# A new opening for a fused attention and mixture-of-experts kernel: three moved steps ahead of and inside the first head

## The chip, the cores and the metric

The kernel runs on one core of a Trainium2 chip. The metric is the time of one execution on the device in microseconds (us), lower being better. TensorE (PE in the views; PEld is its weight loads) multiplies, VectorE (DVE), ScalarE (ACT) and GpSimd (POOL) do the rest, and SyncE (SP) issues the loads and stores.

## The reference

```python
# attention: 4 batches x 8 heads, 576 positions, head size 64, block-causal mask (block 64)
scores = (1 / np.sqrt(D)) * np.matmul(q, k.transpose(0, 1, 3, 2))
scores = np.where(block_i >= block_j, scores, -1000000000.0)
attn = np.exp(scores - np.max(scores, axis=-1, keepdims=True))
attn = attn / (np.sum(attn, axis=-1, keepdims=True) + 1e-09)
x = np.matmul(attn, v)                       # -> 2304 tokens of 512
# first expert layer, dense; its weights arrive as 64-bit floats' bits
x = (((x @ w1) * (x @ w2)) @ w3) @ w_out
# second layer: 8 experts of (512 x 1024, 1024 x 512), the best 2 of them per token
noisy_logits = x @ w_gate + np.log1p(np.exp(x @ w_noise)) * noise
...
out[mask] += top2_w[mask, k, None] * (np.maximum(x[mask] @ w1[e], 0.0) @ w2[e])
```

The weights of the first layer (w1, w2, w3, w_out) are stored as 64-bit numbers. The kernel turns them into 32-bit ones with three integer instructions of VectorE.

## The kernel before, in words

The program has three parts that overlap: attention, one head after the other (32 heads, numbered from 0); the first expert layer in nine chunks of 256 tokens; and the second layer by expert. Precise products are made of three fast ones: each factor is split into a high part (ScalarE, a cast) and a low part (VectorE, what the cast left out).

**A head.** `prep_h` makes Q and K ready: `hi` on ScalarE (L612 for Q, L615 for K), the low part of Q on VectorE (L614), the low part of K, `kl`, on VectorE (L617). `s_unit` multiplies them into score banks `sb` on TensorE (L644, L647 with `kl`, L646 adds the mask by a small product of `mkl` and `mkr`). `s_max` takes the negated row maxima `nm` on VectorE (L658; L661 joins the two of the last tile), and ScalarE exponentiates (L663, into `pb`). `g_unit` transposes `pb` on TensorE (L677), and copies it into `pt` on ScalarE (L681); from head 8 on VectorE makes the low part of `pt` as well (L683). `av_a` and `av_b` multiply by V (L690, L702), the result `ev` is copied (L692, L705) and stored. Score tiles 0 and 1 share a bank, tiles 2 and 3 have one each, and tile 4 has two halves of 288 columns.

**Weights of the first layer.** There are 23 pieces. Each is loaded into `stg` (two buffers), converted into `stf` by `conv64` (L548, L549, L550; one buffer), and then split into a piece `pc` (cast on ScalarE L477, low part on VectorE L481). `feed` does one step of this: it splits the piece that was converted last and converts the next.

**Filler on TensorE.** Between the steps of a head stand the products of the first layer. First w3 times w_out is made from pieces (`w_unit`, 64 units of three 128x512 matmuls, `m<-pc,pc`), then the chunks (`m<-xh,pc` with w1 and w2, later `m<-pc,gt`). All are issued by L486, L487 and L488. A unit can run only when its pieces have been split; the chunks need all the w1 and w2 pieces, which are the last to be converted.

**Order.** Head i's second half and head i+1's first half are written as a list of steps in a string, `FIRST` for i below 10 and `LATER` after it: `s0` to `s3` are scores, `c` is `feed`, `f2.9` asks for 2.9 us of filler, `g`, `a`, `b` are the second half, `h` prepares the head after next, `v` and `l` load. The loop begins with i = -1, where only the first half exists. A scheduler then lays the instructions out on each engine's queue, by priorities and by what it thinks will be ready; filler and `feed` have low priority. An engine runs its queue in order.

Of the kernel before, what the change touches and what calls it, by code (L numbers as in the profile page):

```python
# [14 lines left out]
OP = mybir.AluOpType  # L15
AX = mybir.AxisListType.X
# [46 lines left out]
ZC, NF = 3, 10  # L63
# [4 lines left out]


FIRST = "g0 g1 t f2.9 c t o g2 g3 t p s0 t t s1 s2 f2.9 c t a f2.9 t b0 t s3 h t t c b1 v l"  # L70
LATER = "g0 g1 f2.6 o g2 p t c g3 t t t s0 s1 s2 t c t a f2.6 s3 b0 t t c f2.6 c t b1 h v l"


# [4 lines left out]
def r32(ap):  # L78
    return ap.bitcast(F32)
# [385 lines left out]
class Kernel:  # L465
# [88 lines left out]
    def attention(self):  # L554
        tc, nc, a = self.tc, self.nc, self.a
        moe1 = self.moe1
        stgs = ExitStack()
        with tc.tile_pool(name="p1", bufs=1, side="right") as p1, \
# [3 lines left out]
            mk32 = p1.tile([P, 2, P], F32, name="ev")  # L562
            mkl = p1.tile([P, P], BF16, name="mkl")
            mkr = p1.tile([P, 64], BF16, name="mkr")
# [8 lines left out]
            def buf(h, shape, dt, name):  # L573

                return (px if h < H and h % 2 else p1).tile(shape, dt, name=name)
# [33 lines left out]
            def prep_h(h):  # L609
                c = hd[h]  # L610
                c.hi = buf(h, [P, 2, S], F32R, "hi")
                nc.scalar.activation(c.hi[:, 0, :], c.qk[:, 0, :], AF.Copy, scale=0.125)  # L612
                lo = c.hi[64:128, 0, :]
                nc.vector.scalar_tensor_tensor(lo, c.qk[64:128, 0, :], 0.125, r32(lo), op0=OP.mult, op1=OP.subtract)  # L614
                nc.scalar.copy(c.hi[:, 1, :], c.qk[:, 1, :])  # L615
                c.kl = buf(h, [P, S], F32R, "kl")
                (nc.vector if h < NF - 1 else nc.gpsimd).tensor_tensor(c.kl, c.qk[:, 1, :], r32(c.hi[:, 1, :]), op=OP.subtract)  # L617

            def prep_v(h):
                c = hd[h]  # L620
# [29 lines left out]
            def s_max(h):  # L650
                c = hd[h]
                pb = pbs[h < H and h % 2]
                ex = []
                for t, parts in c.tiles:
                    nm = p1.tile([P, 3], F32, name=f"nm{t}")
                    for n, (o, k0, w) in enumerate(parts):
                        w = min(w, KW[t])
                        nc.vector.tensor_reduce(nm[:, n:n + 1], o[:, 0:w], axis=AX, op=OP.max, negate=True)  # L658
                        ex.append((t, n, o[:, 0:w], k0, nm[:, 2:3] if len(parts) > 1 else nm[:, 0:1]))
                    if len(parts) > 1:  # L660
                        nc.vector.tensor_reduce(nm[:, 2:3], nm[:, 0:2], axis=AX, op=OP.min)  # L661
                for t, n, src, k0, nm in ex:
                    nc.scalar.activation(pb[t][:, k0:k0 + src.free_size()], src, AF.Exp, bias=nm, scale=1.0,  # L663
                                         accum_out=sums[:, h // H, t + n, h % H:h % H + 1])
# [55 lines left out]
            wst = {}  # L720
# [43 lines left out]
            raw = []  # L764

            conv = []

            def feed():

                with tc.high_priority(offset=PIECE_PRIO):  # L770
                    feed_half()

            def feed_half():
                if len(conv) > wst.get("split", 0):
                    _, _, i, o, _ = jobs[len(conv) - 1]
                    pc, w = self.pc[i], conv[-1].shape[-1]
                    self.split((pc[:, 0, o:o + w], pc[:, 1, o:o + w]), conv[-1], low="dve")
                    wst["split"] = len(conv)
                    moe1.conv += w // 512
                n = len(conv)  # L780
                if n < len(jobs) and wst.get("n", 0) >= jobs[n][4]:
                    conv.append(self.conv64(raw[n]))
                    if n + 2 < len(jobs):
                        raw.append(self.load64(*jobs[n + 2][:2]))

# [33 lines left out]
            tick = moe1.tick  # L819
            load(0)  # L820
            nc.sync.dma_start(mk32, a["msk"])
            nc.vector.tensor_copy(mkl, mk32[:, 0, :])
            nc.vector.tensor_copy(mkr, mk32[:, 1, 0:64])
            raw += [self.load64(*jobs[n][:2]) for n in range(2)]
            nc.sync.dma_start(self.ident, a["cst"][:, 0:128])
            feed()
            prep_h(0)
            load(1)
            load_v(0)
            feed()  # L830
            feed()

            def step(i, j, op):

# [34 lines left out]
            for i in range(-1, BH):  # L869
                if i == 2:  # L870
                    moe1.setup_load()
                elif i == 3:
                    moe1.setup()
                elif i == H:
                    pxs.close()
                    moe1.p2b = moe1.p2s.enter_context(tc.tile_pool(name="p2b", bufs=1, reuse_waits="tile"))
                if i >= H and moe1.p2c is None and moe1.conv == 40:
                    stgs.close()
                    moe1.p2c = moe1.p2s.enter_context(tc.tile_pool(name="p2c", bufs=1, reuse_waits="tile"))
                for op in (FIRST if i < NF else LATER).split():  # L880
                    step(i, i + 1, op)
            sums_out(B - 1)
            moe1.ready = B
# [243 lines left out]
```

## Time and profile before

| what | value |
|---|---|
| median of 3 runs | 1084.67 us (1081.68 to 1088.02) |
| the profiled execution's own time | 1086.31 us |
| its span, first to last instruction | 1084.5 us |
| TensorE busy | 1044.3 us, 96% |
| VectorE busy | 556.7 us, 51% |
| ScalarE busy | 495.4 us, 46% |
| GpSimd busy | 303.3 us, 28% |
| mean granted TensorE clock | 0.984 of full speed |

The engines' busy times are means over parts with different limits. The span is 1.8 us shorter than the profiled execution's time, and that execution was 1.6 us slower than the median.

### The profile page before, as it was taken

How to read it: one execution, taken by the hardware profiler on the slowest of the kernel's cores; microseconds unless marked ns; L12 is line 12 of the kernel's file. 1: busy time of each engine (PE TensorE's matmuls, PEld its weight loads, DVE VectorE, ACT ScalarE, POOL GpSimd, SP SyncE). 2: the span in 40 equal slices, each digit the busy share in tenths (PEclk: the TensorE clock that was granted, in tenths of full speed). 3: DMA queues.
4: the chain of work that ended last, by engine and by line, in shares of the span. 5: the costliest groups of instructions: out<-in, count | busy, mean ns of one | idle time of the engine just before them, and what ended most of it. 6: DMA issues, size and time to landing. Idle time of an engine off the chain costs nothing.

```text
span 1084.5 us, 17388 instructions
## 1 busy us (share of the span) xinstructions
PE 1044.3 (96%) x6588; PEld 943.4 (87%) x6588; DVE 556.7 (51%) x1211; ACT 495.4 (46%) x1163; POOL 303.3 (28%) x306
## 2 busy tenths in 40 slices
PE   6999898999999999999999999999999999999996
PEld 4787697898999989899999889889898989999885
DVE  7998899585655666443345443533333333434111
ACT  5875566665566656522224332433333333333111
POOL 1000234234342426131444234241413232120211
PEclk9999898999999999999999999999999999999998
DMA  8764877247442554322423355663535445351212
GB/s 278 245 211 164 234 215 165 71 121 160 158 111 80 155 167 92 84 80 59 79 58 113 93 133 154 185 157 98 153 100 146 108 127 127 107 117 31 39 20 33
DMA packets 79106, 136.34 MB, mean 126 GB/s; under 512 B 21181, under 2 KB 46501, under 8 KB 77861
## 3 DMA queue, kind: packets, MB, share of 16 engines
q1 hardware_dynamic: 68901, 113.98, 36.2%
q0 software_dynamic: 10112, 21.16, 10.6%
q8 instruction: 54, 0.88, 0.3%
q14 instruction: 39, 0.32, 0.1%
HBM read 103.92 MB, written 31.19 MB: 125 GB/s over the span
## 4 chain that ended last, share of the span: by engine, by line
PE 84%; DVE 5%; DMA 4%; ACT 2%; issue 2%; POOL 1%; SPq 1%; POOLq 0%; ACTq 0%; DVEq 0%
PE ph L486 13%; PE ph L487 13%; PE ph L488 13%; PE m L486 10%; PE m L488 10%; PE m L487 10%; PE av L702 4%; PE tp L677 4%; PE sb L647 2%; PE sb L644 2%; DMA v<-in_v_dram 1%; PE m L959 1%; DMA stf<-in_m_dram 1%; DVE nm L658 1%; DVE pc L481 1%
## 5 line engine op out<-in xcount | busy, mean ns | idle before, releaser
L486 PE MATMUL m<-xh,pc 128*128 128x256 f32 x576 | 165.7, 291 | 1.1 <-ACT pc L477 1.0
L487 PE MATMUL m<-xh,pc 128*128 128x256 f32 x576 | 163.9, 288 | 0.0
L488 PE MATMUL m<-xh,pc 128*128 128x256 f32 x576 | 163.0, 288 | 0.6 <-DVE pc L481 0.6
L486 PE MATMUL ph<-xt,pc 128*128 128x384 f32 (+1 forms) x512 | 156.8, 309 | 3.7 <-DVE ht L974 2.1
L487 PE MATMUL ph<-xt,pc 128*128 128x384 f32 (+1 forms) x512 | 157.8, 309 | 0.0
L488 PE MATMUL ph<-xt,pc 128*128 128x384 f32 (+1 forms) x512 | 157.6, 308 | 0.0
L974 DVE SCALAR_TENSOR_TENSOR ht<-ph,ht 128x384 fp32r<-128x384 f32 (+1 forms) x128 | 61.8, 489 | 150.5 <-ACT ht L973 147.0
L481 DVE TENSOR_TENSOR pc<-stf,pc 128x1024 fp32r<-128x1024 f32 (+1 forms) x75 | 88.2, 1191 | 93.1 <-ACT pc L477 83.6
L486 PE MATMUL ph<-pc,ht 128*128 128x512 f32 x320 | 126.0, 395 | 0.0
L488 PE MATMUL ph<-pc,ht 128*128 128x512 f32 x320 | 124.6, 390 | 0.0
L487 PE MATMUL ph<-pc,ht 128*128 128x512 f32 x320 | 124.5, 390 | 0.0
L1001 POOL DMA_INDIRECT out_dram<-yo,ids x40 | 66.5, 1661 | 207.1 <-ACT yo L997 105.8
L973 ACT ACTIVATE ht<-ph 128x384 fp32r<-128x384 f32 (+1 forms) x128 | 55.0, 438 | 136.7 <-PE ph L488 133.9
L486 PEld LDWEIGHTS m<-xh,pc 128*128 128x128 f32 x576 | 111.7, 195 | 2.4 <-ACT pc L477 1.2
L663 ACT ACTIVATE pb<-sb,nm 128x288 f32<-128x288 f32 (+3 forms) x192 | 94.1, 500 | 39.1 <-DVE nm L658 14.4
L487 PEld LDWEIGHTS m<-xh,pc 128*128 128x128 f32 x576 | 111.0, 194 | 0.6
L488 PEld LDWEIGHTS m<-xh,pc 128*128 128x128 f32 x576 | 110.5, 194 | 1.0 <-DVE pc L481 0.8
L481 POOL TENSOR_TENSOR gt<-at,gt 128x256 fp32r<-128x256 f32 x72 | 59.3, 828 | 149.3 <-ACT gt L477 149.0
L486 PEld LDWEIGHTS ph<-xt,pc 128*128 128x128 f32 x512 | 96.5, 189 | 4.7 <-DVE ht L974 2.3
L487 PEld LDWEIGHTS ph<-xt,pc 128*128 128x128 f32 x512 | 96.9, 189 | 0.5 <-DVE xt L481 0.2
L488 PEld LDWEIGHTS ph<-xt,pc 128*128 128x128 f32 x512 | 97.0, 189 | 0.0
L477 ACT CAST pc<-stf 128x1024 fp32r<-128x1024 f32 (+1 forms) x75 | 74.9, 1018 | 44.4 <-DMA stf<-in_m_dram 31.7
(159 smaller groups left out, 2162.1 us busy)
## 6 DMA issues: line engine op xcount, KB each, us to landing
stf<-in_m_dram SPq DMA_DIRECT2D x52, 512.0 KB
qk<-in_qk_dram SPq DMA_DIRECT2D x31, 576.0 KB
stg<-in_w_dram SPq DMA_DIRECT2D x14, 1024.0 KB
x<-ev SPq DMA_DIRECT2D x32, 288.0 KB
xab<-x SPq DMA_DIRECT2D x20, 256.0 KB
yt<-y SPq DMA_DIRECT2D x18, 260.0 KB
v<-in_v_dram SPq DMA_DIRECT2D x24, 160.0 KB
out_dram<-cst SPq DMA_DIRECT2D x3, 1280.0 KB
```

What stands on the lines that cost most here:

```text
L477: d = nc.scalar.copy(h, src)
L481: return d, eng.tensor_tensor(l, src, r32(h), op=OP.subtract)
L486: nc.tensor.matmul(out, a, c, start=first, stop=False)
L487: nc.tensor.matmul(out, a, d, start=False, stop=False)
L488: nc.tensor.matmul(out, b, c, start=False, stop=last)
L644: nc.tensor.matmul(o, lh, c.hi[:, 1, k0:k0 + w], start=True, stop=False)
L663: nc.scalar.activation(pb[t][:, k0:k0 + src.free_size()], src, AF.Exp, bias=nm, scale=1.0, accum_out=sums[:, h // H, t + n, h % H:h % H + 1])
L677: nc.tensor.transpose(bank[:, n * P:(n + 1) * P], pb[t][:, kt * P:(kt + 1) * P], self.ident)
L702: nc.tensor.matmul(c.av[:, o0:o0 + w], c.vv[:, kt, :], c.pt[:, i, s0:s0 + w], start=(kt == 0 and i == 0), stop=(kt == 4 and i == m - 1))
L973: a = nc.scalar.activation(hh[:, 0, f, :], ph, AF.Relu)
L974: v = nc.vector.scalar_tensor_tensor(hh[:, 1, f, :], ph, 0.0, r32(hh[:, 0, f, :]), op0=OP.max, op1=OP.subtract)
L1001: nc.gpsimd.indirect_dma_start(out=self.a["out"], out_offset=self.idx(e, i), in_=yo, in_offset=None, compute_op=OP.add)
```

## The change

Three things are moved, and nothing is removed.

- K's low part of head 0 comes ahead of the two casts of the mask (`mkl`, `mkr`) on VectorE: `issue_after` holds the casts until the instruction that `prep_h` returns.
- The first `conv64` is held until the last row maximum that was written before it, which is the second one of head 0.
- The three `feed` calls ahead of the loop are gone, and the first iteration (i = -1) runs a list of its own, `START`, with seven `feed` steps where it had three and three more in `FIRST`. It asks for no filler; `FIRST` asked for it three times there.

```diff
+START = "s0 c c s1 c c s2 c s3 c c h b1 v l"
...
-                (nc.vector if h < NF - 1 else nc.gpsimd).tensor_tensor(c.kl, c.qk[:, 1, :], r32(c.hi[:, 1, :]), op=OP.subtract)
+                return (nc.vector if h < NF - 1 else nc.gpsimd).tensor_tensor(c.kl, c.qk[:, 1, :], r32(c.hi[:, 1, :]), op=OP.subtract)
...
-                        nc.vector.tensor_reduce(nm[:, n:n + 1], o[:, 0:w], axis=AX, op=OP.max, negate=True)
+                        wst["max"] = nc.vector.tensor_reduce(nm[:, n:n + 1], o[:, 0:w], axis=AX, op=OP.max, negate=True)
...
-                    conv.append(self.conv64(raw[n]))
+                    with ExitStack() as es:
+                        if n == 0:
+                            es.enter_context(tc.issue_after(wst["max"].ins))
+                        conv.append(self.conv64(raw[n]))
...
-            nc.vector.tensor_copy(mkl, mk32[:, 0, :])
-            nc.vector.tensor_copy(mkr, mk32[:, 1, 0:64])
             raw += [self.load64(*jobs[n][:2]) for n in range(2)]
             nc.sync.dma_start(self.ident, a["cst"][:, 0:128])
-            feed()
-            prep_h(0)
+            with tc.issue_after(prep_h(0).ins):
+                nc.vector.tensor_copy(mkl, mk32[:, 0, :])
+                nc.vector.tensor_copy(mkr, mk32[:, 1, 0:64])
             load(1)
             load_v(0)
-            feed()
-            feed()
...
-                for op in (FIRST if i < NF else LATER).split():
+                for op in (START if i < 0 else FIRST if i < NF else LATER).split():
```

The changed file has one line more from L71 on, so L617 of before is L618 of the change, and so on. The scheduler lays out a different order from the first head to the end of attention; the second expert layer's order is the same.

**The opening.** On VectorE, from the low part of Q of head 0 on, before:

```order
L614 SCALAR_TENSOR_TENSOR hi<-qk,hi 64x576
L822 CAST mkl<-ev 128x128
L823 CAST mkr<-ev 128x64
L617 TENSOR_TENSOR kl<-qk,hi 128x576
L548 TENSOR_SCALAR stf<-stg 128x512
L549 SCALAR_TENSOR_TENSOR stf<-stg,stf 128x512
L658 TENSOR_REDUCE nm_185<-sb 128x1
L658 TENSOR_REDUCE nm_187<-sb 128x1
L550 SCALAR_TENSOR_TENSOR stf<-stg,stf 128x512
L658 TENSOR_REDUCE nm_195<-sb 128x1
L658 TENSOR_REDUCE nm_202<-sb 128x1
L481 TENSOR_TENSOR pc_70<-stf,pc_70 128x512
```

The same place in the change, from `kl` on; the last row belongs to the head after (`hi` of head 1), and the second half of head 0's last tile (`nm_220` once more) comes right behind it:

```order
L618 TENSOR_TENSOR kl<-qk,hi 128x576
L829 CAST mkl<-ev 128x128
L830 CAST mkr<-ev 128x64
L659 TENSOR_REDUCE nm_155<-sb 128x1
L659 TENSOR_REDUCE nm_157<-sb 128x1
L549 TENSOR_SCALAR stf<-stg 128x512
L659 TENSOR_REDUCE nm_179<-sb 128x1
L550 SCALAR_TENSOR_TENSOR stf<-stg,stf 128x512
L659 TENSOR_REDUCE nm_202<-sb 128x1
L551 SCALAR_TENSOR_TENSOR stf<-stg,stf 128x512
L659 TENSOR_REDUCE nm_220<-sb 128x1
L615 SCALAR_TENSOR_TENSOR hi<-qk,hi 64x576
```

The first two maxima now stand ahead of the first conversion, and the low part of head 1's Q stands ahead of the last maximum of head 0; the low part of the first piece (`pc_70`) stood there earlier, and is now seven rows further down. On ScalarE, from head 0's first exponential on, before:

```order
L663 ACTIVATE pb_107,sums<-sb,nm_185 128x128
L663 ACTIVATE pb_108,sums<-sb,nm_187 128x192
L477 CAST pc_70<-stf 128x512
L663 ACTIVATE pb_109,sums<-sb,nm_195 128x320
L663 ACTIVATE pb_110,sums<-sb,nm_202 128x448
L612 ACTIVATE hi<-qk 128x576
L615 CAST hi<-qk 128x576
```

And in the change:

```order
L664 ACTIVATE pb_107,sums<-sb,nm_155 128x128
L664 ACTIVATE pb_108,sums<-sb,nm_157 128x192
L664 ACTIVATE pb_109,sums<-sb,nm_179 128x320
L613 ACTIVATE hi<-qk 128x576
L616 CAST hi<-qk 128x576
L664 ACTIVATE pb_110,sums<-sb,nm_202 128x448
L478 CAST pc_70<-stf 128x512
```

The casts of head 1's Q and K moved ahead of the exponential of head 0's 448 columns, and the first piece's cast moved behind it.

**From w3 and w_out to the first chunk.** On TensorE, at the last `w_unit` (`m<-pc_69,pc_71` is its last row), before:

```order
L487 MATMUL m<-pc_69,pc_71 128x512
L488 MATMUL m<-pc_69,pc_71 128x512
L644 MATMUL sb<-hi 128x288
L647 MATMUL sb<-kl,hi 128x288
L702 MATMUL av<-pt,vv 128x320
L644 MATMUL sb<-hi 128x288
L646 LDWEIGHTS mkl
L646 MATMUL sb<-mkr,mkl 128x64
L647 MATMUL sb<-kl,hi 128x288
L690 MATMUL tp<-pt,vv 128x128 x2
```

Before, 38 rows of attention stand between the last `w_unit` and the first matmul of a chunk. In the change there are eight:

```order
L489 MATMUL m<-pc_69,pc_71 128x512
L678 MATMUL tp<-ident,pb_109 128x128
L678 MATMUL tp<-ident,pb_110 128x128
L678 MATMUL tp<-ident,pb_111 128x128
L678 MATMUL tp<-ident,pb_107 128x128
L703 MATMUL av<-pt,vv 128x448 x2
L678 MATMUL tp<-ident,pb_110 128x128
L678 MATMUL tp<-ident,pb_111 128x128 x2
L703 MATMUL av<-pt,vv 128x448
L487 MATMUL m<-xh,pc_72 128x256
```

The filler of the two kinds now nearly meets, since the `w_unit`s moved about one head later.

**The last conversion.** On VectorE, around the low part of the 23rd piece (`pc_69`), before; `nm_2065` is the last maximum of head 13:

```order
L658 TENSOR_REDUCE nm_2065<-sb 128x1
L692 COPY ev<-tp 128x128
L614 SCALAR_TENSOR_TENSOR hi<-qk,hi 64x576
L661 TENSOR_REDUCE nm_2065<-nm_2065 128x1
L481 TENSOR_TENSOR pc_69<-stf,pc_69 128x1024
```

In the change, where `nm_2358` to `nm_2375` belong to head 15:

```order
L659 TENSOR_REDUCE nm_2358<-sb 128x1
L659 TENSOR_REDUCE nm_2360<-sb 128x1
L659 TENSOR_REDUCE nm_2368<-sb 128x1
L659 TENSOR_REDUCE nm_2375<-sb 128x1
L684 TENSOR_TENSOR pt<-tp,pt 128x512
L482 TENSOR_TENSOR pc_69<-stf,pc_69 128x1024
```

The last piece now comes between one and two heads later on VectorE's queue. Up to it VectorE has 10 more maxima of scores (two of each of the widths 128, 192, 320, 448 and 288), 7 more low parts of `pt` (four of 448, two of 512, one of 384), and one each of L614, L661 and L692; nothing is taken away. TensorE, up to the first matmul that needs the piece, has 23 more transposes, 16 more matmuls of scores and 7 of the mask, 20 more of `av` and 4 of L690, and equally many of filler.

## Rows read from the trace of the kernel before

**Rows 1.** The page: busy us, share of the span, instructions of TensorE and VectorE.

```profile
PE 1044.3 (96%) x6588; PEld 943.4 (87%) x6588; DVE 556.7 (51%) x1211; ACT 495.4 (46%) x1163; POOL 303.3 (28%) x306
```

**Rows 2.** Windows: stretch, length, busy us by engine, granted clock, DMA share, GB/s.

```profile
0.00:5.20 5.20, 0.01 (x1) 0.04 (x1) 1.36 (x3) 2.64 (x3) 2.65 (x18) 1.00 0.58 181
5.20:25.00 19.80, 14.74 (x56) 10.59 (x57) 16.90 (x33) 11.63 (x34) 2.61 (x4) 1.00 0.94 301
25.00:50.00 25.00, 23.36 (x140) 18.05 (x139) 23.51 (x45) 20.23 (x56) 0.00 (x0) 1.00 0.73 243
50.00:100.00 50.00, 50.00 (x275) 40.09 (x274) 44.05 (x71) 35.12 (x90) 0.00 (x0) 1.00 0.61 201
100.00:200.00 100.00, 89.74 (x560) 77.87 (x559) 89.25 (x139) 60.50 (x156) 28.90 (x22) 0.91 0.72 187
200.00:300.00 100.00, 98.55 (x712) 91.00 (x711) 63.48 (x185) 61.82 (x180) 35.81 (x34) 0.98 0.48 132
```

**Rows 3.** Timeline of VectorE, opening: start, us, line, shapes, [idle before <-releaser].

```profile
6.21 0.75 DVE L617 TENSOR_TENSOR kl<-qk,hi 128x576 fp32r<-128x576 f32 x1
8.53 0.43 DVE L548 TENSOR_SCALAR stf<-stg 128x512 int32<-128x512 int32 x1 [1.57 <-DMA stg<-in_w_dram]
...
9.60 0.55 DVE L658 TENSOR_REDUCE nm<-sb 128x1 f32<-128x128 f32 x2
...
16.43 0.14 DVE L661 TENSOR_REDUCE nm<-nm 128x1 f32<-128x2 f32 x1
```

**Rows 4.** Timeline of ScalarE, opening.

```profile
12.63 0.69 ACT L612 ACTIVATE hi<-qk 128x576 fp32r<-128x576 f32 x1
...
15.05 0.68 ACT L612 ACTIVATE hi<-qk 128x576 fp32r<-128x576 f32 x1 [1.17 <-DMA qk<-in_qk_dram]
```

**Rows 5.** Timeline of TensorE: the first scores, and heads 1, 3 and 4's 448 columns.

```profile
7.56 1.11 PE L647 MATMUL sb<-kl,hi 128*128 128x192 f32 x3
...
19.14 0.57 PE L644 MATMUL sb<-hi 128*128 128x448 f32 x1
...
41.06 0.37 PE L644 MATMUL sb<-hi 128*128 128x448 f32 x1
...
48.39 0.37 PE L644 MATMUL sb<-hi 128*128 128x448 f32 x1
```

**Rows 6.** Windows of 10 and 20 us, columns as in the second group.

```profile
120.00:130.00 10.00, 6.95 (x42) 5.75 (x41) 8.77 (x14) 6.71 (x17) 2.30 (x2) 0.91 0.91 214
130.00:140.00 10.00, 8.37 (x37) 6.85 (x37) 8.56 (x14) 6.57 (x16) 3.76 (x4) 0.57 0.84 248
...
160.00:180.00 20.00, 15.80 (x104) 13.34 (x103) 19.84 (x30) 13.37 (x37) 10.56 (x7) 0.90 0.69 160
```

**Rows 7.** Timeline of TensorE: last `w_unit`, first matmul of a chunk.

```profile
122.13 0.39 PE L488 MATMUL m<-pc,pc 128*128 128x512 f32 x1
...
135.28 0.63 PE L486 MATMUL m<-xh,pc 128*128 128x256 f32 x2
```

**Rows 8.** Timeline of VectorE: the low part of the last piece.

```profile
186.38 1.66 DVE L481 TENSOR_TENSOR pc<-stf,pc 128x1024 fp32r<-128x1024 f32 x1 [0.56 <-ACT pc L477]
```

**Rows 9.** Groups of VectorE, 100 to 190 us: count | busy, mean ns | idle before.

```profile
L683 DVE TENSOR_TENSOR pt<-tp,pt 128x448 fp32r<-128x448 f32 x11 | 6.6, 611 | 0.0
L658 DVE TENSOR_REDUCE nm<-sb 128x1 f32<-128x288 f32 x11 | 4.9, 446 | 1.2 <-PE sb L647 1.1
```

**Rows 10.** Chain that ended last, in order of time: eight transposes (start, us).

```profile
39.92 0.87 PE tp L677 x8
```

**Rows 11.** Timeline of TensorE: score matmuls, `av` and transposes back to back.

```profile
122.35 0.29 PE L644 MATMUL sb<-hi 128*128 128x288 f32 x1
122.48 0.29 PE L647 MATMUL sb<-kl,hi 128*128 128x288 f32 x1
...
123.32 0.76 PE L702 MATMUL av<-pt,vv 128*128 128x320 f32 x5
123.92 0.51 PE L677 MATMUL tp<-ident,pb 128*128 128x128 f32 x3
```

## The prediction

> **What bounds the kernel now.** I read the page's busy times first [rows 1]: TensorE is busy 1044.3 of 1084.5 us and no other engine much over half, so this looks like a kernel with 40 us to win at most. That share is a mean over stages, so the windows come next [rows 2]. From 200 us on TensorE is full (98.6 of 100 us) and VectorE has room (63 of 100). The change cannot help there; whatever TensorE work is left at 200 us is simply carried out. Ahead of 200 us it is another kernel. TensorE is idle for all of the first 5.2 us, for 5.1 of the next 19.8, for 1.6 of the next 25, and for 10.3 between 100 and 200, where its granted clock also averages 0.91. VectorE in that time is nearly full: 23.5 of 25, 44.1 of 50, 89.3 of 100 us, which is 156.8 of 175 or 90%. So up to the last weight piece two engines bind together. What the change is worth is the TensorE idle time ahead of the point at which the last piece's low part is there, 186.4 us [rows 8], plus what the clock takes.
>
> **The opening.** Before, the first conversion stands ahead of the first two maxima on VectorE and waits for its load until 8.53 us, with the engine idle for 1.57; the maxima follow at 9.60 [rows 3]. The scores that they read were being made from 7.0 to 8.4 (the low K part ended at 6.96, the last group of three matmuls starts at 7.56 [rows 3, 5]). In the change the casts of the mask still wait for the mask's load, so the first matmul of the mask is where it was, and `kl`, 0.75 us, no longer stands behind them: the matmuls with `kl` can start about 0.5 us earlier. The two maxima then run at about 7.7, some 1.9 us earlier than at 9.60. That gain does not last. ScalarE's queue now has head 1's Q and K ahead of head 0's exponential of 448 columns, and they need head 1's load. When it lands the trace only bounds: not after 12.63, when ScalarE takes it without waiting, and not before 8.5, since it is queued behind the first weight loads; head 2's lands just before 15.05 [rows 4]. By bytes, 512, 64 and 576 KB of the 2048 KB that land from 8.5 to 15.05, it is 8.5 + 6.5 x 1152 / 2048 = 12.2, an estimate. Then the two casts take 1.2 and the exponential of 448 columns starts at 13.4, where it had ended ahead of 12.63 before, and VectorE, whose queue has head 1's low Q part ahead of head 0's last maximum, waits until 12.9, then does 0.76 + 0.45 + 0.75 + 0.14 and ends head 0's maxima at 15.0 instead of 16.43. So head 0 is 1.4 us earlier, but VectorE has done 2.2 us less by then (the first piece's low part and most of a second conversion lie behind that point now). If heads bind, that is -1.4; if VectorE's work binds, it is +0.8. I take the middle, **-0.3**.
>
> **What lies ahead of the last piece.** This is the largest part of the change, and the diff doesn't show it. VectorE gets 10 more maxima ahead of the last piece, at the 446 ns of the 288 wide ones, which are the middle width: 4.5 us; 7 low parts of `pt`, at the 611 ns of the 448 wide ones: 4.3 [rows 9]; and one low Q part like the 0.75 us of `kl`, one small maximum of 0.14 [rows 3] and one copy, together 1.0. The sum is 9.8 us. TensorE gets, ahead of the matmul that waits for it, 23 transposes and 4 of L690 at 0.11 (eight take 0.87) [rows 10], 16 score matmuls at the 0.13 between two starts of the 288 wide ones, seven 64-column ones of the mask (0.3 in all, at a third of that), and 20 of `av`, of which 16 go at 0.12 (five in the 0.60 from 123.32 to 123.92) and four, of 448 columns, at 0.13 x 448 / 288 = 0.2 [rows 11]: 2.9 + 2.1 + 0.3 + 2.7 = 8.0 us. Attention has moved ahead of the piece on both engines. At equal stalls the piece comes 9.8 us later, and TensorE has used 8.0 of it: **+1.8** idle. If VectorE keeps its 90%, the 9.8 become 10.9 and with the 0.8 from the opening it is +3.7; if the waits of both engines shrink in the new order it is 0 or less.
>
> **A hole that closes.** Before, the last `w_unit` starts at 122.13 and the first matmul of a chunk at 135.28 [rows 7]. In the 13 us between them TensorE has only attention; in the two windows it is idle for 3.05 and 1.63, and the granted clock falls to 0.57 in the second [rows 6]. At 0.57 the 8.37 busy us hold some 3.6 that full clock would not need, so the hole costs up to 4.7 + 3.6 = 8.3 us. The new order puts the last `w_unit` eight rows ahead of the first chunk's matmul, so the hole should close. But TensorE can only keep what VectorE's queue allows. VectorE was idle for 2.7 of those 20 us, against 0.2 of the 20 from 160 to 180 [rows 6], so its work can come 2.5 us earlier at most, and the rest of the 8.3 turns up again as waits for pieces ahead of the last one. I take **-2.5**; the bounds are 0 and -8.3.
>
> **The sum.** -0.3 + 1.8 - 2.5 = -1.0 us on the profiled execution's 1086.3 (a span of 1084.5 and 1.8 around it), thus 1085.3; that execution was 1.6 over the median of the runs shown, so the forecast is **1083.7**. Costed at nothing: the later loads of pieces (SyncE issues them when a conversion frees its buffer; TensorE has attention to do in the meantime) and the first iteration's missing requests for filler, since a unit that is not placed there is placed later, and TensorE has to run it anyway. If that cover is gone and TensorE waits for pieces instead, the price is that of the second rival.
>
> **A rule on the clock.** The rows show two speeds of TensorE: a 448-column score matmul takes 0.57 us at 19.14 and 0.37 at 41.06 and 48.39 [rows 5], and in the hole, after 3 us of waits in ten, the granted clock fell to a mean of 0.57, near its lower level of 1.2 GHz [rows 6]. The windows' clock column reads 1.00 in the first 25 us all the same, so I go by the durations there. The Trainium skill, "TensorE: Matmul & The Clock Gate", section "HAM oscillation — how this bites in real kernels", says that a kernel whose matmuls stand between waits has its clock throttled again and again, and pays at half rate for each; by that, less filler in the first heads would speak against this change, and the third rival would be its outcome. The trace bears it out at 130 us and not in heads 3 and 4, which have no filler of their own between 41.06 and 48.39 and run fast.
>
> **Rivals.**
> *The hole closes whole.* Conversions pack more tightly once attention is less in their way, VectorE has no more idle time from 107 to 187 than in its best 20 us, and 5.8 more of the 8.3 us come back: 1083.7 - 5.8 = 1077.9. For it: VectorE at 19.84 of 20 from 160 to 180 [rows 6]. Against it: TensorE was idle for 4.2 of those 20 us itself, so a tight VectorE queue does not yet feed it. Chance 0.20.
> *VectorE's queue alone decides.* The last piece comes 10.9 + 0.8 later, TensorE has 8.0 for it: 1084.7 + 3.7 = 1088.4, within the measurement. It also stands for the change that does nothing that it says after the first microseconds. Chance 0.22.
> *The slow one.* With eight `w_unit`s fewer up to head 6, TensorE sits between waits for the first heads and stays at the lower level for longer. A head without filler is 48.39 - 41.06 = 7.3 us with about 0.5 of waits in it, so 6.8 of work [rows 5], and one head more at half rate costs 6.8: 1083.7 + 6.8 = 1090.5. It decides from about 6.5 us of full-rate work on that is done at half rate. For it: the opening ran at half rate until after 19.14. Against it: in heads 3 to 4 the level held. Chance 0.18.
> The forecast has 0.40.
>
> **How the numbers follow.** 0.5% is 5.4 us, and that is about what a measurement of this kernel can tell from no change: the three runs lie 6.3 us apart. The forecast and the second rival are within it, 0.62. The first rival is faster, 0.20; the third slower, 0.18. The range goes from below the first rival, 1076, to the slow one, 1091; what is left out is a hole that closes in full with an opening at its best, and two heads or more at half rate.
>
> **What would show it.** In the profile after: the first maxima at 7.6 to 8.0 instead of 9.60; an idle ScalarE until about 12.2 and the 448-column exponential near 13.4; head 0's L662 near 15.0; the last piece's low part at 192 to 198 instead of 186.4; no 13 us without filler around the first chunk's matmul, with the clock at 1.00 there; TensorE's idle time from 100 to 200 us between 7 and 12 us, with the waits nearer to the end of that stretch. The forecast is wrong if 448-column matmuls take 0.57 us later than 30 us, if the last piece is there by 190, or if TensorE waits after 200 us for anything that it did not wait for before.

## The result and the profile after

The changed kernel takes 1097.88 us (median of 4, 1095.49 to 1098.86), the kernel before 1084.88 us beside it: ratio 1.0126, 95% interval 1.0106 to 1.0145. It is slower by 13 us, outside the range 1076 to 1091 and on the side that had a chance of 0.18. The profiled execution took 1098.86 us with a span of 1097.0.

The windows of the changed kernel, with the columns of [rows 2]; the last two rows cut the stretch that lost:

```profile
5.20:25.00 19.80, 15.23 (x68) 11.20 (x69) 15.46 (x34) 12.62 (x36) 2.39 (x4) 1.00 0.85 261
25.00:50.00 25.00, 24.58 (x144) 18.89 (x145) 22.93 (x47) 21.89 (x62) 0.00 (x0) 1.00 0.69 228
100.00:200.00 100.00, 80.08 (x477) 67.92 (x475) 84.11 (x125) 54.95 (x144) 23.52 (x19) 0.90 0.69 184
200.00:300.00 100.00, 95.82 (x653) 86.82 (x654) 66.72 (x153) 58.42 (x162) 32.94 (x30) 0.97 0.45 124
...
150.00:200.00 50.00, 34.82 (x226) 29.64 (x224) 38.99 (x59) 27.21 (x75) 11.88 (x11) 0.86 0.58 148
250.00:300.00 50.00, 47.43 (x326) 42.63 (x325) 30.30 (x85) 28.72 (x81) 17.82 (x17) 0.98 0.51 135
```

Up to 50 us TensorE is idle for 1.7 us less than in [rows 2] (4.57 and 0.42 against 5.06 and 1.64): the opening won there. From 100 to 200 it is idle for 19.9 us against 10.3, and from 200 to 300 for 4.2 against 1.5. The same two cuts of the kernel before show where:

```profile
150.00:200.00 50.00, 44.58 (x303) 40.07 (x302) 43.76 (x71) 32.97 (x89) 17.78 (x13) 0.93 0.60 142
250.00:300.00 50.00, 48.55 (x330) 44.10 (x329) 32.54 (x92) 29.77 (x89) 17.56 (x16) 0.97 0.56 155
```

In 150 to 200 us the change carries out 226 matmuls, the kernel before 303. The idle time there grew from 5.4 to 15.2 us. The waits of ScalarE, VectorE and TensorE in the change from 160 to 200 us (us in total, times, longest) name what came last:

```profile
ACT vv L625 <- DMA v<-in_v_dram: 9.1, 1, 9.1
...
PE tp L678 <- ACT pb L664: 8.5, 1, 8.5
...
DVE nm L659 <- PE sb L648: 5.0, 1, 5.0
DVE stf L549 <- DMA stg<-in_w_dram: 3.4, 1, 3.4
```

The chain is to be read from the top: ScalarE stands at the copy of V, all of head 13's exponentials stand behind it, TensorE has no transposes to do and VectorE no maxima. Head 12's step on SyncE shows why V is late. It fills tables in DRAM: three DMAs to `idt` and zeros to `yt` (L135 to L150). SyncE's queue in the change, then before (start, us of issue, line):

```profile
165.73 1.41 SPq L135 DMA_DIRECT2D idt<-y  x2
167.18 2.36 SPq L136 DMA_DIRECT2D idt<-lt  x1
169.64 0.55 SPq L540 DMA_DIRECT2D stg<-in_w_dram  x1
170.23 0.62 SPq L148 DMA_DIRECT2D yt<-cst  x1
170.89 7.48 SPq L150 DMA_DIRECT2D yt<-cst  x2
178.47 1.38 SPq L608 DMA_DIRECT2D v<-in_v_dram  x1
179.95 0.55 SPq L540 DMA_DIRECT2D stg<-in_w_dram  x1
```

```profile
165.13 0.55 SPq L539 DMA_DIRECT2D stg<-in_w_dram  x1
...
172.99 1.41 SPq L134 DMA_DIRECT2D idt<-y  x2
174.44 2.68 SPq L135 DMA_DIRECT2D idt<-lt  x1
177.16 1.09 SPq L147 DMA_DIRECT2D yt<-cst  x1
178.30 1.02 SPq L149 DMA_DIRECT2D yt<-cst  x2
179.41 0.60 SPq L607 DMA_DIRECT2D v<-in_v_dram  x1
```

Before, the tables come when the last weight load (165.13) has been issued, and ScalarE is ready for the V behind them only at 186.8: it waits 0.45 us. After, attention is ahead of the weights, head 12 is reached 7 us earlier, and the tables stand ahead of two weight loads and of a V that ScalarE wants at 176.3. SyncE is held for 7.48 us at two issues that took 1.02, V is issued at 178.47 and used at 185.46. That is no later than before, where V is issued at 179.41 and used at 187.22; what differs is that ScalarE stands ready for it 10 us earlier. In the stretch 178 to 186 TensorE does nothing at all, and its clock falls to the lower level:

```profile
178.00:182.00 4.00, 0.00 (x0) 0.00 (x0) 0.90 (x3) 0.00 (x0) 0.00 (x0) 0.59 0.96 299
182.00:186.00 4.00, 0.00 (x0) 0.00 (x0) 0.69 (x1) 0.54 (x2) 0.00 (x1) 0.50 1.07 373
```

The Trainium skill, "DMA: Bandwidth & Descriptors", section "Queues, rings and completion order", says that a DMA issued by SyncE goes to rings in which descriptors are consumed in order. The trace agrees: 1024 packets of 12 bytes and 1002 of 8 start between 168 and 170 us, the 2048-byte packets of the weight load issued behind them from 170 on, and V's 1280-byte packets from 182 on.

So the **theory** after the result: the held first conversion lets attention run ahead of the weight pieces, and the tables of head 12 thereby overtake loads that TensorE needs. **Rivals**: the order of attention and pieces costs by itself (on VectorE, or because TensorE has too little chunk work to cover its waits); another part of the change (START) costs.

### The profile page after: what moved, and what is told of

It reads as the page before. It is cut to its first block, busy times and chain, and to the rows that moved or that the text cites. A ratio compares the mean times of both kernels' runs of the same rounds, so it can differ in the third digit from the quotient of the medians.

```text
span 1097.0 us, 17401 instructions
## 1 busy us (share of the span) xinstructions
PE 1046.5 (95%) x6588; PEld 943.2 (86%) x6588; DVE 564.2 (51%) x1211; ACT 494.0 (45%) x1163; POOL 297.9 (27%) x306
## 4 chain that ended last, share of the span: by engine, by line
PE 76%; ACT 1%; DMA 1%; DVE 1%; SPq 1%; issue 1%; POOL 0%; POOLq 0%; ACTq 0%
PE ph L487 13%; PE ph L488 13%; PE ph L489 13%; PE m L487 9%; PE m L489 9%; PE m L488 9%; PE tp L678 2%; PE av L703 2%; PE sb L645 1%; PE sb L648 1%; PE m L960 1%; PE m L245 1%; DMA v<-in_v_dram 1%; PE m L236 1%; PE m L253 0%
## 5 line engine op out<-in xcount | busy, mean ns | idle before, releaser
L664 ACT ACTIVATE pb<-sb,nm 128x320 f32<-128x320 f32 (+3 forms) x192 | 94.0, 499 | 30.0 <-PE tp L678 18.8
L487 PEld LDWEIGHTS ph<-xt,pc 128*128 128x128 f32 x512 | 95.7, 188 | 4.4 <-ACT xt L478 2.1
L659 DVE TENSOR_REDUCE nm<-sb 128x1 f32<-128x128 f32 (+2 forms) x192 | 79.3, 440 | 35.4 <-PE sb L648 33.7
L678 PE MATMUL tp<-ident,pb 128*128 128x128 f32 x480 | 80.5, 279 | 17.1 <-ACT pb L664 13.4
```

The costliest lines, as they stand in the source:

```text
L487: nc.tensor.matmul(out, a, c, start=first, stop=False)
L659: wst["max"] = nc.vector.tensor_reduce(nm[:, n:n + 1], o[:, 0:w], axis=AX, op=OP.max, negate=True)
L678: nc.tensor.transpose(bank[:, n * P:(n + 1) * P], pb[t][:, kt * P:(kt + 1) * P], self.ident)
```

## The experiments

"Ratio" is to the kernel before, run beside each, with its 95% interval. It is estimated from all executions and can differ a little from the quotient of two medians (a_rows: 1091.43 and 1083.27 would give 1.0075).

| run | edit, to the kernel | ratio | median us |
|---|---|---|---|
| a_no_hold | change, first conversion not held | 1.0004 (0.9988 to 1.0020) | 1083.64 |
| a_no_kl | change, casts ahead of K's low part | 1.0061 (1.0041 to 1.0082) | 1090.49 |
| a_tables13 | change, tables at head 13 | 1.0035 (1.0020 to 1.0049) | 1087.34 |
| b_tables11 | before, tables at head 11 | 1.0045 (1.0029 to 1.0061) | 1088.47 |
| a_tables15 | change, tables at head 15 | 1.0083 (1.0057 to 1.0109) | 1092.06 |
| a_tables_poolq | change, tables issued by GpSimd | 1.0106 (1.0082 to 1.0131) | 1095.67 |
| a_idt13 | change, `idt` at head 13, `yt` at 12 | 1.0039 (1.0024 to 1.0053) | 1087.79 |
| b_start_tables15 | a_no_hold, tables at head 15 | 1.0065 (1.0043 to 1.0087) | 1090.55 |
| a_rows | change, tables in rows | 1.0061 (1.0042 to 1.0081) | 1091.43 |
| a_rows_pool | a_rows, late low parts on GpSimd | 1.0057 (1.0036 to 1.0079) | 1088.66 |
| b_start_rows | a_no_hold, tables in rows | 1.0008 (0.9993 to 1.0022) | 1084.92 |
| b_start_rows_pool | the same, late low parts on GpSimd | 0.9952 (0.9931 to 0.9973) | 1078.50 |
| b_pool | before, late low parts on GpSimd | 0.9948 (0.9931 to 0.9965) | 1078.40 |
| a_rows_backheads | a_rows, heads held to the pieces | 0.9964 (0.9951 to 0.9977) | 1080.22 |
| a_backheads | change, heads held to the pieces | 0.9959 (0.9945 to 0.9973) | 1079.40 |
| a_rows_back_pool | a_rows_backheads, low parts on GpSimd | 0.9996 (0.9979 to 1.0013) | 1083.12 |

### Which part of the change

a_no_hold:

```
-                    with ExitStack() as es:
-                        if n == 0:
-                            es.enter_context(tc.issue_after(wst["max"].ins))
-                        conv.append(self.conv64(raw[n]))
+                    conv.append(self.conv64(raw[n]))
```

> The changed kernel without the hold of the first conversion: START and K's low part ahead of the casts stay. From head 2 on VectorE's and SyncE's orders are those of the kernel before. Theory: 1082-1087 us, no stall at 178-186, the last weight unit near 122 and the first chunk matmul near 135 as before. Rival (START, which alone drops the calls of the first three conversions, is the loss): 1094-1099 us.

Measured 1.0004. Without the hold, START and K's low part ahead of the casts change nothing that can be measured; the rival "START" by itself is out. a_no_kl keeps START and the hold:

```
+            nc.vector.tensor_copy(mkl, mk32[:, 0, :])
+            nc.vector.tensor_copy(mkr, mk32[:, 1, 0:64])
...
-            with tc.issue_after(prep_h(0).ins):
-                nc.vector.tensor_copy(mkl, mk32[:, 0, :])
-                nc.vector.tensor_copy(mkr, mk32[:, 1, 0:64])
+            prep_h(0)
```

> The changed kernel without its first part: the mask's casts stand ahead of K's low part again; START and the held first conversion stay. In the program written out, the table DMAs then stand behind the last weight loads again, as in the kernel before. Theory (table DMAs overtaking are the loss): 1083-1089 us, and the wait for V at 180-186 is not there. Rival (the hold and the order it leads to cost by themselves on VectorE): 1094-1099 us. The third (the held conversion moves the whole weight schedule, some of it costs): 1089-1094 us.

Measured 1.0061 (1090.49 us), in the third case: the held conversion moves the weights, and some of that costs. Here the tables do stand behind the last weight loads, ScalarE waits for V for 0.8 us, and the kernel is still 7 us slower. So the hold is the part that costs, and not through the tables alone; K's low part, worth nothing without the hold, decides with it whether the tables come ahead. The hold was not run without START.

### Moving the tables

a_tables13, and b_tables11 the other way round:

```
-                    if i == 12:
+                    if i == 13:
```

> The changed kernel with one edit: the step that fills the tables in DRAM (idt and the rows of yt) is issued at head 13 in place of head 12, so its DMAs stand behind the last two weight loads and behind head 13's V on SyncE's queue, as they stood in the kernel before. Theory (those DMAs, ahead of V and of two weight loads, are the loss): TensorE's idle time at 150-200 falls from 15.2 us to 4-7 us, ScalarE's wait for V (9.1 us) goes, time 1082-1088 us, most likely 1085. Rival (the order of attention and conversions on VectorE is the loss): the time stays at 1094-1099 us with the idle time at 150-200 above 12 us, because VectorE's order is all but that of the changed kernel. Rival (the clock alone): the idle time falls but the half-clock stretches stay, 1090-1095 us.

> The kernel before with one edit: the tables are filled at head 11 in place of head 12, so that their DMAs stand ahead of one V load and of the last weight loads on SyncE's queue, as they do after the change. Theory: the stall of the changed kernel appears in the kernel before: a wait for V on ScalarE of 5-9 us and all engines idle for 3-7 us near 165-180, time 1090-1098 us. Rival (the order on VectorE is the loss, the tables are hidden): 1083-1087 us, within 0.3% of before.

The first gives back 0.9 of the 1.26%: theory right on the wait for V, but the idle time at 150 to 200 is 9.3 us, not the 4 to 7 expected. Windows of a_tables13:

```profile
150.00:200.00 50.00, 40.70 (x270) 35.22 (x269) 47.18 (x71) 30.74 (x84) 16.44 (x12) 0.93 0.65 165
250.00:300.00 50.00, 47.39 (x335) 42.53 (x334) 31.47 (x80) 31.05 (x88) 17.53 (x16) 1.00 0.56 149
```

b_tables11 puts the stall into the kernel before: 1.0045, some 5 us, less than expected and between its two cases. ScalarE's waits in it, 160 to 200 us:

```profile
ACT vv L624 <- DMA v<-in_v_dram: 4.1, 1, 4.1
```

The tables cost where a V that is wanted soon stands behind them, with no part of the change in the kernel. Is it a collision again at head 13? In a_tables13 the Q and K of a later head were issued at 176.28, between the table DMAs, and ScalarE got them at 187.82, after a wait of 1.04. Two runs at head 15, with and without the hold (edit as above, `15`):

> The changed kernel with the table step issued at head 15, later than the run that issued it at head 13 (1.0035 of before) and where its DMAs also stand behind head 15's Q and K load. What is left of the loss then is either a collision of the tables with that load (in the run at head 13, ScalarE waited 1.0 us for it and TensorE 2.2 us behind it) or VectorE's queue with the later conversions. If the collision: 1081-1085 us, and no wait for a load of Q, K or V over 1 us in 160-210. If VectorE's queue: 1085-1089 us, with TensorE's lost time at 150-200 still 4 us above that of the kernel without the hold, and TensorE's waits there for hi, which VectorE writes.

> START and K's low part ahead of the casts, no hold of the first conversion, and the table step at head 15. Without the table move this kernel took 1.0004 of before. Theory: the tables cost something in the kernel before too (ScalarE waited 0.5 us for V at 187, the clock fell at 176), 1079-1083 us, ratio 0.996-0.999. Rival: behind the weight loads they are hidden already, 1083-1085 us, ratio 1.000.

Both are slower than with the tables at head 13, or where they were, and both expectations missed. In the second a new wait took the place of the old one. ScalarE's waits, 165 to 260 us:

```profile
ACT lt L248 <- DMA idt<-lt: 7.0, 1, 7.0
```

The buffer `lt`, from which the table is written, is used again by the first chunk, and this reader is late. What the first of the two lost isn't settled; it shows no such wait in 200 to 300, but TensorE is idle for 3.8 us at 250 to 300.

a_tables_poolq and a_idt13 were to tell which DMAs block, and where:

```
-                nc.sync.dma_start(dst, src)
+                nc.gpsimd.dma_start(dst, src)
```

```
-                    if i == 12:
+                    if i in (12, 13):
...
+        if step == 0 and part == 0:
+            self.y_zeros(NT - CH, CH // P + 1)
```

> The changed kernel with the table DMAs issued at head 12 as in it, but by GpSimd instead of SyncE: V and the last weight loads no longer stand behind them on SyncE's queue, while the DMA engines get the same table work at the same time. If it is SyncE's queue that costs: the wait for V is under 2 us and the time is 1085-1090 us. If it is the DMA engines, filled with table packets: V still lands late and the time stays at 1093-1100 us.

> The changed kernel with the table step cut in two: the zeros of yt stay at head 12, the three DMAs to idt are issued at head 13. If the DMAs to idt (the third writes 4-byte elements) are what blocks: SyncE's 7 us at the yt zeros are gone and the time is 1086-1090 us, near the run with all tables at head 13. If the zeros of yt block by themselves: 1094-1099 us as in the changed kernel.

The first doesn't tell: on GpSimd's queue nothing held the DMAs, so the writes to `idt` went out from 3.29 us on, and head 1's Q and K arrived late. The opening of a_tables_poolq on ScalarE:

```profile
17.80 0.68 ACT L614 ACTIVATE hi<-qk 128x576 fp32r<-128x576 f32 x1 [8.08 <-DMA qk<-in_qk_dram]
```

In the change that instruction starts at 12.83: the same writes, 5.0 us lost elsewhere. The second run came out as expected, 1.0039: the zeros of `yt` are harmless at head 12 (SyncE issued the two large ones in 1.23 us), the writes to `idt` are not. (The third of these writes goes out in 104 packets of 512 bytes in the change's trace, not in 4-byte elements as the expectation has it.)

### Are the pieces too small?

The two writes `idt<-y` go out as 1024 pieces of 12 and 1024 of 8 bytes (128 partitions, 8 tables, 3 or 2 numbers of 4 bytes). a_rows writes the same values from rows that lie together, at the same places of the queue:

```
-        nc.gpsimd.iota(self.tr0, pattern=[[0, E], [0, NSLOT]], base=NT, channel_multiplier=1)
+        nc.gpsimd.iota(self.tr0[0:E, 0:384], pattern=[[1, P], [0, 3]], base=NT, channel_multiplier=0)
...
-            for dst, src in k.slots(tab, self.tr0):
-                nc.sync.dma_start(dst, src)
+            nc.sync.dma_start(tab[:, 0:512], self.tr0[0:E, :])
+            nc.sync.dma_start(tab[:, 512:CAP], self.tr0[32:32 + E, 384:512])
```

> The changed kernel with the table step at head 12 and every DMA at its place on SyncE's queue; only the source of the first tables is laid out in rows, so that the two writes to idt that had 1024 pieces of 12 and of 8 bytes each become 8 pieces of 2048 and 8 of 512 bytes with the same values. Theory (thousands of small pieces fill the DMA engines ahead of V): the stall at 178-186 goes though nothing moved on the queue, ScalarE's wait for V falls under 2 us, 1085-1089 us, ratio 1.001-1.005. Rival (SyncE's order alone, whatever the pieces): 1093-1099 us as in the changed kernel.

SyncE's queue in a_rows, and what the DMA queue moved from 170 to 178 us in the change and then in a_rows (packets, MB, share of the time of 16 engines):

```profile
167.49 0.62 SPq L150 DMA_DIRECT2D yt<-cst  x1
168.16 1.30 SPq L152 DMA_DIRECT2D yt<-cst  x2
169.94 0.58 SPq L610 DMA_DIRECT2D v<-in_v_dram  x1
```

```profile
q1 hardware_dynamic: 267, 0.31, 70.2%
```

```profile
q1 hardware_dynamic: 1779, 1.82, 77.9%
```

The mechanism is right: with no DMA moved, V is issued 8.5 us earlier, and ScalarE waits for it 0.5 us instead of 9.1. Behind the small pieces a packet took 8 x 16 x 0.702 / 267 = 0.34 us, in a_rows 8 x 16 x 0.779 / 1779 = 0.056. But the time, 1.0061, is above the range expected. With the stall gone, 6.6 us are still lost. In b_start_rows, without the hold, the rows are worth nothing:

> START and K's low part ahead of the casts, no hold, tables in rows. Without the rows this kernel took 1.0004 of before. If the small pieces cost the kernel before something too: 1079-1082.5 us, ratio 0.995-0.999. If they are hidden there: 1083-1085 us.

Measured 1.0008: where a V stands behind the tables that nobody waits for, their cost is hidden. It is there all the same: in the kernel before, too, the packets behind the small pieces are slow (74 of 1024 bytes that start between 180 and 182 us took 0.5 us each).

### What the hold costs without the stall

If VectorE is the bound, fewer of its instructions should help. The low part of the pieces from the 19th on goes to GpSimd:

```
-                    self.split((pc[:, 0, o:o + w], pc[:, 1, o:o + w]), conv[-1], low="dve")
+                    self.split((pc[:, 0, o:o + w], pc[:, 1, o:o + w]), conv[-1], low="dve" if len(conv) < 19 else "pool")
```

> The run before (tables in rows) with the low part of the pieces from the 19th on given to GpSimd: some 5 instructions of 1.2 us less on VectorE at 155-200. Theory for what is left of the loss (VectorE's queue is the bound there, with the later conversions): TensorE's lost time at 150-200, about 17 us in the runs with the hold and 12 without, falls by 2-5 us; 1082-1086 us. Rival (GpSimd takes 2.4 us for such an instruction and TensorE then waits for it, or VectorE is slowed beside it): 1086-1092 us.

> The same with the low part of the pieces from the 19th on on GpSimd. If VectorE is the bound at 150-190 without the hold too: 1078-1082 us. If not, or if GpSimd is late: 1083-1088 us.

> The kernel before with one edit: the low part of the pieces from the 19th on is given to GpSimd. If VectorE at 155-190 bounds the kernel before and START and the tables in rows add nothing: 1077-1081 us, ratio 0.994-0.997, as in the run with START and rows (0.9952). If the three only help together: 1081-1085 us.

With the hold it brings nothing that can be told (1.0057 against 1.0061), though VectorE is busy for 41.4 of the 50 us from 150 to 200 instead of 45.5. TensorE is idle there for 8.3 us instead of 7.7, 1.0 of it a wait for a low part from GpSimd. Without the hold it brings 0.5%, and b_pool shows that START and rows have no part in that. So VectorE's load is not most of what is left of the loss (each ratio is known to 0.2%); here my theory fell. The other candidate is the order. Counted in the traces, up to head 14's 448-column score matmul TensorE had carried out 189 chunk matmuls (`m<-xh`) before and in a_no_hold, and 124 in the change and in a_rows. If that is the cause, the waits of heads 11 to 14 have that much less to cover them. a_rows_backheads holds the heads back:

```
                 elif kind == "h" and j + 1 < BH:
-                    prep_h(j + 1)
+                    with ExitStack() as es:
+                        if 10 <= j + 1 < 17:
+                            es.enter_context(tc.issue_after(wst["pieces"][-6].ins))
+                        prep_h(j + 1)
```

> The changed kernel with tables in rows, and with heads 10 to 16 held back on VectorE: the high and low parts of Q and K of each wait for the low part of the sixth last piece that has been written so far. In the program the last seven pieces then stand behind 10, 11, 12, 13, 13 and 14 finished heads, as in the kernel before (11, 11, 12, 13, 14), not 12 to 15. If attention ahead of the pieces is what is left of the loss: TensorE's lost time at 150-200 falls from 19.0 us to 11-15 us and the time to 1083-1088 us, ratio 1.000-1.004. If not: 1089-1094 us, as without it (1.0061).

"Lost time" in it is a stretch less the matmuls that start in it, each counted with the lower quartile of the times from one start to the next of its shape in that profile; so it holds idle time and slow clock together. It fell at 150 to 200 from 19.0 to 13.5 us, and the count up to head 14 rose to 168. The ratio is 0.9964. Three windows of a_rows (the profile is of its slowest execution, 1092.91 us), then of a_rows_backheads:

```profile
100.00:150.00 50.00, 44.53 (x249) 37.69 (x248) 43.76 (x64) 27.76 (x70) 11.66 (x9) 0.93 0.78 212
150.00:200.00 50.00, 42.27 (x264) 37.06 (x263) 45.50 (x65) 29.11 (x78) 16.59 (x13) 0.86 0.55 169
250.00:300.00 50.00, 47.56 (x309) 42.74 (x308) 27.36 (x72) 27.49 (x78) 16.25 (x15) 0.93 0.53 143
```

```profile
100.00:150.00 50.00, 42.14 (x241) 35.88 (x240) 43.74 (x57) 23.97 (x56) 11.43 (x8) 0.96 0.79 221
150.00:200.00 50.00, 43.68 (x294) 37.94 (x293) 46.64 (x77) 35.21 (x97) 19.93 (x15) 0.97 0.49 154
250.00:300.00 50.00, 49.74 (x359) 45.75 (x358) 34.20 (x97) 31.94 (x92) 16.47 (x16) 1.00 0.55 149
```

VectorE is not less busy than in a_rows (46.6 against 45.5), TensorE carries out 30 more matmuls from 150 to 200 and 50 more from 250 to 300, and its granted clock is up there from 0.86 to 0.97 and from 0.93 to 1.00. The stretch at 250 to 300 was part of the loss too (lost time 8.8 us in a_rows, 3.0 here), and I had not looked for its cause in the order. Holding the heads back has a price at 100 to 150, where TensorE is idle for 7.9 us instead of 5.5. So from 100 to 200 it is idle no less than in a_rows (14.2 and 13.2 us): what rose in that stretch is the clock (0.90 to 0.97).

That the order costs, this run shows. How it costs is only argued: in a_no_kl TensorE has 166 chunk matmuls behind it at the same point, about as many as here, no V is late, and yet it loses 20.1 us from 150 to 200. One head earlier a_no_kl stands at 124 and this run at 144, so the count at one head doesn't settle it.

The last two ask how much of the whole the order explains (the tables untouched), and whether the two gains add up. The edits are those above:

> The changed kernel with heads 10 to 16 held back to the pieces as in the run before, tables as they were, at head 12. Holding head 12 back also brings the table DMAs behind all weight loads and behind head 13's V and head 14's Q and K in the program, as in the kernel before. If the order of heads and pieces is the root of both parts of the loss (the tables overtake because head 12 comes early): 1079-1084 us, ratio 0.996-1.000, no wait for V over 2 us. If the small pieces block whatever stands around them: 1085-1090 us.

> Tables in rows, heads 10 to 16 held back, and the low part of the pieces from the 19th on given to GpSimd. If the two edits relieve different waits: 1073-1078 us, ratio 0.990-0.995. If they relieve the same (VectorE between heads 11 and 16): 1077-1082 us, ratio 0.995-0.998.

a_backheads is the changed kernel with this one edit, and it takes 0.9959: the whole loss is gone and 0.4% won, since holding head 12 back also puts the tables behind the weight loads (the last of these is issued at 168.44, the tables from 174.46 on, and ScalarE waits 0.2 us for V). Its windows:

```profile
150.00:200.00 50.00, 44.54 (x300) 40.00 (x301) 47.31 (x77) 36.23 (x98) 18.85 (x15) 0.93 0.61 156
250.00:300.00 50.00, 49.74 (x359) 45.76 (x358) 33.32 (x95) 32.68 (x93) 16.74 (x16) 1.00 0.55 145
```

By lost time, 150 to 250 is back near the level of the kernel before (15.9 us against 14.8), and 250 to 300 is below it (2.9 against 6.0). The same hold of the heads was not tried on the kernel before, so how much of the result is repair and how much a gain of its own isn't shown.

The gains don't add up: with both, 0.9996, a miss. In that profile (1079.99 us, the fastest of its executions) TensorE waits 2.2 us for low parts from GpSimd; why the median lies 3 us higher isn't settled.

## Why the prediction was wrong

**The opening: right, its gain too small and not kept.** The first maxima start at 7.57 (7.6 to 8.0 was written), head 1's load holds ScalarE until 12.83 (12.2), the 448-column exponential starts at 13.98 (13.4), head 0's maxima end at 15.49 (15.0). VectorE's rows in the change:

```profile
7.57 0.56 DVE L659 TENSOR_REDUCE nm<-sb 128x1 f32<-128x128 f32 x2 [1.18 <-PE sb L648]
...
13.54 0.76 DVE L615 SCALAR_TENSOR_TENSOR hi<-qk,hi 64x576 fp32r<-64x576 f32 x1 [1.75 <-ACT hi L613]
...
15.49 0.15 DVE L662 TENSOR_REDUCE nm<-nm 128x1 f32<-128x2 f32 x1
```

The term was -0.3; TensorE's idle time up to 50 us fell by 1.7, beyond the bound of -1.4. By lost time it is 2.0 less up to 50 us and 1.7 more from 50 to 100. The two add up to the -0.3 of the forecast, but that is luck: the term was the middle of two bounds and knew of no loss behind 50 us, and what causes that loss wasn't examined. The slow rival didn't come in its form: a 448-column matmul takes 0.37 us at 27.20 already.

**The hole: closed where it was said, but the idle time came back beside it.** The last `w_unit` starts at 127.94, the first chunk matmul at 129.55. In the change:

```profile
120.00:130.00 10.00, 9.91 (x45) 8.11 (x46) 8.88 (x14) 4.43 (x12) 0.06 (x1) 0.83 1.10 265
130.00:140.00 10.00, 8.00 (x57) 7.03 (x56) 9.88 (x16) 6.74 (x18) 2.79 (x2) 0.89 0.74 196
```

Idle 2.1 us against 4.7 in [rows 6], thus -2.6, where -2.5 was taken; the clock was to be 1.00 there and is 0.83 and 0.89. Around these 20 us TensorE now waits for what it did not before, so that from 100 to 150 the idle time is the same, in the change and then before:

```profile
100.00:150.00 50.00, 45.25 (x254) 38.28 (x252) 45.12 (x67) 27.74 (x70) 11.64 (x9) 0.93 0.81 219
100.00:150.00 50.00, 45.16 (x259) 37.80 (x258) 45.49 (x69) 27.53 (x67) 11.12 (x9) 0.90 0.84 231
```

The clock is a little higher, and by lost time the stretch gains 1.7 us.

**Attention ahead of the last piece: the right place, too small a size.** The term was +1.8 with a bound of +3.7. In a_tables13, where no V is late, the idle time at 150 to 200 is 9.3 against 5.4: +3.9. The mechanism was only half right: it was costed as VectorE work against TensorE work, but relieving VectorE in a_rows_pool brought nothing and putting the order back in a_rows_backheads brought all of it. Whether it acts by the chunk work that TensorE has between its waits isn't shown. The stretch behind 200 us, where the idle time went from none to 1.6 us up to 250 and from 1.5 to 2.6 up to 300, was in no term.

**The step that failed: "Costed at nothing: the later loads of pieces".** It looked at the loads of pieces alone and had TensorE covered by attention. But attention that comes earlier brings its own DMAs forward, and one step of it, head 12's, puts the tables on SyncE's queue. They passed two weight loads and went ahead of a V that attention itself wanted 10 us earlier (176.3 against 186.8). So the work that was to hide the late loads was what stopped, for 8.5 us, and the clock fell with it. By lost time the change has 11.5 us more than before at 150 to 200, 3.5 more at 200 to 250 and 1.1 more at 250 to 300, against the +1.8 of the sum; with the tables moved to head 13 the 11.5 are 6.0. By the ratios the tables make 0.65 (a_rows) to 0.9 (a_tables13) of the 1.26%; the rest is the mis-sized +1.8. The price given for that case, the second rival's 1088.4, was too low as well, since that rival has only VectorE's lag in it. All that I listed of the moved work was instructions of VectorE and TensorE; the queue that they were moved past was SyncE's.

**What would show it.** The last piece was to be there at 192 to 198 and came at 209.80; the idle time from 100 to 200 was to be 7 to 12 us and is 19.9; and TensorE does wait after 200 us for what it did not before. The first two lie outside what was written, and the third is one of the signs by which the text called itself wrong, rightly. A 448-column matmul of 0.57 us comes later than 30 us too, among others at 187.73, behind the stop; as a sign of a slow opening it says nothing, since the kernel before has a slow one at 130 us.

## What to carry to other kernels

When an edit lets one stream of work run ahead of another, list every DMA that this stream issues and see on each queue what they now overtake; a rare step (a table filled once) counted for more here than the steady ones. A stall that goes when you move its last releaser shows what sat there, not why it came there: moving or mending the tables gave back a third (head 15) to three quarters (head 13) of the loss, putting the order of heads and pieces right gave back all of it. When the likely bound is "a busy engine", relieve it once: here VectorE at 94% (47.2 of 50 us in a_tables13) was, as far as a_rows_pool can tell, not what TensorE lacked most.

## What was not expected of the hardware

- 20 KB of table in 2048 pieces of 8 and 12 bytes, with a weight load behind them, held SyncE's next issues for 7.48 us, and the packets from 170 to 178 us took 0.34 us each, against 0.056 with the same values in 16 pieces. In the kernel before, with no weight load behind them, the same issues took 1.02 us. The Trainium skill, "DMA: Bandwidth & Descriptors", section "Why small descriptors are slow (HBM only)", gives a fixed cost for each small packet. Byte for byte the trace bears that out: a 12-byte packet took 9 ns, a 2048-byte one 87 ns at 182 to 184 us. But all but 22 of the small ones had started by 170; that the packets behind them took 0.5 to 0.7 us each (2048 bytes, 172 to 178 us), the runs show and don't explain.
- The same writes to `idt`, issued by GpSimd from 3.29 us on, delayed head 1's Q and K by 5.0 us.
- A stop of TensorE of 8.5 us brings the granted clock to 0.50 in 182 to 186.
